# Splitting the state-space part of a fused layer into two column halves, and interleaving the phases of the halves

## The chip, the cores and the metric

One core of one Trainium2 chip. The metric is device microseconds of one execution. The kernel before takes 2095 to 2099 us (medians); executions of one kernel scatter by some 0.5%.

In the profile, PE is TensorE's matmuls, PEld its weight loads, DVE is VectorE, ACT is ScalarE, POOL is GpSimd and SP is SyncE, whose queue issues most transfers.

## The reference, cut to what matters

Forward and backward of a layer with two parallel branches on one normalised input, 2048 tokens wide 576 columns. All gradients are outputs.

```python
def _A_ref(u, ...):                       # state-space branch, N = 128, D = 576, L = 2048
    P = jnp.exp(logdA[:, :, None] * l[None, None, :])
    K = jnp.einsum("dn,dnl,dn->dl", Cc, P, dB).real
    ...                                   # y = irfft(rfft(u) * rfft(K)), plus u * Dskip
def _B_ref(x, W_gate, W_up, W_down):      # feed-forward branch, F = 4608
    gate = einsum(x, W_gate); up = einsum(x, W_up)
    return einsum(relu(gate) * up, W_down)
xn = _layernorm(x)
return x + _A_ref(xn, ...) + _B_ref(xn, ...)
# reference() returns the output and its vjp for all inputs
```

The state-space branch ("S4" below) treats every one of the 576 columns by itself. That is why it can be cut into two halves of 288 columns. The feed-forward branch ("FFN") is nearly all matmuls.

## The kernel before: the parts that the change and the argument touch

The FFN is a Python generator that yields an estimate of its own time after each piece. S4 is a second generator. The driver pulls S4 along so that its yields stay at `PACE` times those of the FFN. What is emitted earlier has priority; the compiler's scheduler then fixes each engine's order.

```python
PACE = 0.95
for us in ffn.gen(ln, final):
    ...
    ft += us
    while s4_open and stt < PACE * (ft - start):
        r = next(sgen, None)
        ...
        stt += r

def gen(self):                            # S4
    yield from self.phase1()              # transforms of signal and gradient -> dk
    yield from self.phase2()              # kernel K and its gradient sums: exp, sin, small matmuls
    yield from self.phase3()              # parameter gradients, transforms of K, products, transforms back
```

Phase 2 works on 144 groups of four columns; one group:

```python
v.tensor_tensor(E[:], ..., op=ALU.mult)
v.tensor_tensor(ya[:], ..., op=ALU.mult)
v.tensor_scalar(yr[:], ya[:], MAGIC, None, op0=ALU.add)
v.scalar_tensor_tensor(yr[:], yr[:], MAGIC, ya[:], op0=ALU.subtract, op1=ALU.subtract)
nc.scalar.activation(sn[:], yr[:], ACT.Sin, scale=-TWO_PI)
nc.scalar.activation(ya[:], yr[:], ACT.Abs)
nc.scalar.activation(cs[:], ya[:], ACT.Sin, scale=-TWO_PI, bias=g.hpcol[:])
v.tensor_tensor(Y[:, 0], Ef, cs[:], op=ALU.mult)
v.tensor_tensor(Y[:, 1], Ef, sn[:], op=ALU.mult)
...   # then 8 small matmuls, 8 transposes, 8 small matmuls, evictions, sums
```

The FFN's weight gradients read rows of the gradient (`gq`) and of the input (`xs`), in two buffers each:

```python
self.dp = pool("ffn_d", 2)
gq = self.dp.tile([P, ST, 144], BF16, name="gq")       # in dw_down, four per chunk
xs = self.dp.tile([P, ST, P], BF16, name="xs")         # in dw_gu and dw_left, five per chunk
```

## Time and profile before

| | before |
|---|---|
| time, median of 5 | 2095.1 us (2093.5 to 2102.7) |
| PE busy | 1870 us, 89% of the span |
| DVE, ACT busy | 1468 and 1465 us, 70% each |
| clock granted to PE | 0.968 |
| DMA packets, HBM | 239 thousand, 174 GB/s |

How to read it: no engine is full over the whole span, but each is nearly full somewhere. The page's slices, the table of stretches, the matmuls' true pace and PE's waits are in the prediction, which shows them line by line and works out that 1715 us of TensorE work are needed and some 378 us are lost.

### The profile page before, as it was taken

Reading aid. Unit: us, or ns where it says so; the run is one execution under the profiler, and the core shown is the slowest. Engines: PE = TensorE matmul, PEld = TensorE weight load, DVE = VectorE, ACT = ScalarE, POOL = GpSimd, SP = SyncE. Lnnn points to the kernel's source line nnn. Section 1 sums busy time; section 2 is a strip of 40 time slices with the busy share of each in tenths; the row PEclk is TensorE's granted clock in tenths of the full one; section 3 lists DMA queues with packets and bytes.
Section 4 is the critical chain, followed back from the end, with each engine's and each line's share of the span. In section 5 each row is a group of like instructions: output and inputs, shape, how many; then the busy total and the mean of one; then the engine's idle time right before and its main releaser. Section 6 shows DMA issues by size and latency. Waiting matters only on the chain.

```text
span 2092.8 us, 45262 instructions
## 1 busy us (share of the span) xinstructions
PE 1870.3 (89%) x17723; PEld 1279.1 (61%) x17723; DVE 1468.5 (70%) x3424; ACT 1465.3 (70%) x3187; POOL 263.3 (13%) x321
## 2 busy tenths in 40 slices
PE   6989999876899999989999999999898998899786
PEld 3655567544566666766666666666665674566455
DVE  6454555279999888898989878897356765741563
ACT  3665665468989988988979979888646762452562
POOL 4210100021111201201201101201101000010110
PEclk8999999987999999999999999999999998999988
DMA  9648789742555644645744735645857896995686
GB/s 306 223 155 297 219 249 290 221 113 53 113 126 119 130 114 108 134 117 109 141 119 108 159 94 109 138 128 99 246 156 228 243 284 240 306 268 149 173 238 185
DMA packets 239472, 366.60 MB, mean 175 GB/s; under 512 B 91866, under 2 KB 156506, under 8 KB 238490
## 3 DMA queue, kind: packets, MB, share of 16 engines
q1 hardware_dynamic: 207898, 297.64, 44.6%
q0 software_dynamic: 29248, 63.72, 19.3%
q8 instruction: 138, 2.26, 0.5%
q10 hardware_dynamic: 2112, 2.36, 0.3%
q14 instruction: 76, 0.62, 0.1%
HBM read 214.45 MB, written 149.20 MB: 174 GB/s over the span
## 4 chain that ended last, share of the span: by engine, by line
PE 37%; ACT 25%; DVE 17%; DMA 14%; issue 6%; SPq 1%; POOL 0%; ACTq 0%; DVEq 0%; POOLq 0%
PE ps_mm L246 8%; PE ps_mm L288 7%; PE ps_mm L322 6%; ACT osx L65 4%; ACT YT L65 3%; PE ps_s L603 3%; PE ps_mm L308 3%; DMA gq<-gq_dram 3%; PE ps_s L604 2%; ACT ysn L767 2%; ACT ycs L769 2%; ACT ya L768 2%; PE pt L270 2%; ACT hN L65 2%; DMA bC<-C_dk 1%
## 5 line engine op out<-in xcount | busy, mean ns | idle before, releaser
L65 ACT CAST osx<-ps_mm 128x288 bf16<-128x288 f32 x721 | 276.2, 438 | 61.8 <-PE ps_mm L288 59.4
L293 POOL DMA_DIRECT2D acc_dram<-osx x176 | 152.8, 871 | 1194.3 <-ACT osx L65 925.4
L288 PE MATMUL ps_mm<-wgT,dgT 128*128 128x288 bf16 x1152 | 218.2, 291 | 13.9 <-DVE upm L253 8.4
L288 PE MATMUL ps_mm<-wuT,duT 128*128 128x288 bf16 x1152 | 216.1, 290 | 0.0
L322 PEld LDWEIGHTS <-xs 128*128 128x128 bf16 x1536 | 147.9, 98 | 99.5 <-DMA xs<-xs_dram 5.4
L246 PE MATMUL ps_mm<-gT,wdT 128*128 128x512 bf16 x720 | 192.8, 386 | 10.0 <-DVE upm L253 10.0
L246 PE MATMUL ps_mm<-xT,wg 128*128 128x512 bf16 x720 | 199.8, 384 | 1.1 <-ACT osx L65 0.7
L308 PE MATMUL ps_mm<-gq,hN 128*128 128x144 bf16 x2304 | 172.6, 231 | 28.7 <-DMA gq<-gq_dram 28.7
L288 PE MATMUL ps_mm<-wd,hT 128*128 128x288 bf16 x1152 | 189.6, 289 | 8.3 <-ACT osx L65 2.6
L246 PE MATMUL ps_mm<-xT,wu 128*128 128x512 bf16 x720 | 193.1, 382 | 1.6 <-DVE upm L253 1.6
L308 PEld LDWEIGHTS <-hN 128*128 128x128 bf16 x2304 | 157.3, 100 | 37.5 <-DMA gq<-gq_dram 19.8
L253 DVE SCALAR_TENSOR_TENSOR upm<-rg,ps_mm 128x512 bf16<-128x512 bf16 x144 | 98.6, 685 | 112.6 <-PE ps_mm L246 89.1
L65 ACT COPY YT<-ps_s 128x1024 bf16<-128x1024 bf16 x143 | 148.6, 1039 | 17.3 <-PE ps_s L824 16.5
L322 PE MATMUL ps_mm<-dgN,xs 128*128 128x384 bf16 x768 | 144.8, 328 | 4.1 <-DMA xs<-xs_dram 4.1
L65 ACT CAST dhb<-ps_mm 128x512 bf16<-128x512 f32 x144 | 85.8, 596 | 82.4 <-PE ps_mm L246 82.0
L288 PEld LDWEIGHTS <-dgT 128*128 128x128 bf16 x1152 | 112.4, 99 | 46.0 <-issue 18.2
L322 PE MATMUL ps_mm<-duN,xs 128*128 128x384 bf16 x768 | 138.6, 326 | 0.0
L840 DVE TENSOR_TENSOR pr<-X,ps_s 128x256 f32<-128x256 f32 x288 | 110.5, 417 | 33.7 <-PE ps_s L836 33.2
L288 PEld LDWEIGHTS <-duT 128*128 128x128 bf16 x1152 | 113.6, 99 | 32.8 <-issue 2.3
L288 PEld LDWEIGHTS <-hT 128*128 128x128 bf16 x1152 | 108.3, 99 | 41.4 <-issue 8.1
L246 PEld LDWEIGHTS <-wdT 128*128 128x128 bf16 x720 | 70.2, 99 | 83.7 <-issue 14.8
L65 ACT CAST obw<-ps_mm 128x384 bf16<-128x384 f32 x103 | 48.9, 475 | 99.9 <-PE ps_mm L322 82.6
(247 smaller groups left out, 4141.6 us busy)
## 6 DMA issues: line engine op xcount, KB each, us to landing
acc_dram<-osx POOLq DMA_DIRECT2D x192, 288.0 KB, 4.8
gT<-gT_dram SPq DMA_DIRECT2D x44, 640.0 KB, 5.9
xT<-xT_dram SPq DMA_DIRECT2D x44, 640.0 KB, 5.6
gq<-gq_dram SPq DMA_DIRECT2D x48, 576.0 KB, 4.8
xs<-xs_dram SPq DMA_DIRECT2D x48, 512.0 KB, 3.9
A_ug<-fA SPq DMA_DIRECT2D x16, 576.0 KB, 4.1
out_dram<-obw SPq DMA_DIRECT2D x96, 96.0 KB, 2.7
b_ug<-A_ug SPq DMA_DIRECT2D x16, 576.0 KB, 5.6
```

Source lines behind the costliest of these rows:

```text
L65: self.nc.scalar.copy(out, in_)
L246: nc.tensor.matmul(ps[:], lhsT=w[:, k, fs], rhs=rhs[:, k, :], start=(k == 0), stop=(k == NK - 1))
L253: nc.vector.scalar_tensor_tensor(upm[:], rg[:], 0.0, ps_u[:], op0=ALU.is_gt, op1=ALU.mult)
L270: nc.tensor.transpose(out=pt[:, j, :], in_=src[:, j * P:(j + 1) * P], identity=g.ident_bf[:])
L288: nc.tensor.matmul(ps[:, :DH], lhsT=lt[:, js], rhs=rh, start=(i == 0), stop=(i == len(mms) - 1))
L293: nc.gpsimd.dma_start(g.acc_dram[:, t, :, :], o[:], accum_op=ALU.add)
L308: nc.tensor.matmul(ps[:, (ft - f) * 144:(ft - f + 1) * 144], lhsT=self.hN[:, st, ft * P:(ft + 1) * P], rhs=gq[:, st, :], start=(st == 0), ...
L322: nc.tensor.matmul(ps[:, :Fc], lhsT=xs[:, st, :], rhs=src[:, st, :], start=(st == 0), stop=(st == ST - 1))
L603: nc.tensor.matmul(ps[:, :DH], lhsT=CC[:], rhs=src[:, o, hs], start=True, stop=False)
L604: nc.tensor.matmul(ps[:, :DH], lhsT=sm[:], rhs=src[:, other, hs], start=False, stop=True)
L767: nc.scalar.activation(sn[:], yr[:], ACT.Sin, scale=-TWO_PI)
L840: nc.vector.tensor_tensor(pr[:], X[:, dx:dx + DG, r0:r0 + 2].rearrange("p d r a -> p d (r a)").unsqueeze(2).to_broadcast(sh), psg[:, 0:DG ...
```

## The change

Its intent is to spread S4's three phases, which load different engines, more evenly over the FFN. It does five things: (1) cut S4's arrays into halves; (2) mix phase 2 of one half with transforms of the other, and stretch the two pieces that have no partner; (3) write the transform matrices to DRAM and load slices of them; (4) let the row loads share three buffers; (5) shrink other pools to make room. The letters (a) to (e) of the prediction stand for other steps, and it leaves (3) out. The diff, cut to its core:

```diff
-PACE = 0.95
+PACE = 1.1
+W1, W2, W3 = 56.0, 400.0, 91.0
...
-        self.tp = pool("ffn_t", 2 * FTC)
+        self.tp = pool("ffn_t", 2 * FTC - 1)
-        self.dp = pool("ffn_d", 2)
+        self.dp = pool("ffn_d", 3)
...
-        gq = self.dp.tile([P, ST, 144], BF16, name="gq")
+        gq = self.dp.tile([P, ST, 144], BF16, name="rows")
...
-        xs = self.dp.tile([P, ST, P], BF16, name="xs")
-        nc.sync.dma_start(xs[:], g.xs_dram[k][:])
+        xs = self.dp.tile([P, ST, 144], BF16, name="rows")
+        nc.sync.dma_start(xs[:, :, 0:P], g.xs_dram[k][:])
...
-                per = (len(todo) + FTC - 1) // FTC
+                per = (len(todo) + FTC - 2) // (FTC - 1)
...
-        self.A = {1: d("A_k", [P, ST, 1, 2, D]), 2: d("A_ug", [P, ST, 2, 2, D])}
+        two = lambda name, shape: [d(f"{name}{hf}", shape) for hf in range(2)]
+        self.A = {1: two("A_k", [P, ST, 1, 2, DH]), 2: two("A_ug", [P, ST, 2, 2, DH])}
...   # phase1, phase2, phase3 become p1(hf), p2(hf, pools), p3(hf) on DH = 288 columns;
...   # dkc and yr get one buffer, YT two; the products of two spectra work in place
+    def both(self, a, wa, b, wb):
+        ta = tb = 0.0
+        for us in a:
+            ta += us
+            yield us
+            while b is not None and tb * wa < ta * wb:
+                r = next(b, None)
+                ...
+                    tb += r
+                    yield r
...
     def gen(self):
-        yield from self.phase1()
-        yield from self.phase2()
-        yield from self.phase3()
+        self.make_dft16()
+        yield 1.0
+        yield from self.make_dft128()
+        yield from self.params()
+        with ExitStack() as c:
+            pools = self.p2_pools(c)
+            for us in self.p1(0):
+                yield 2.5 * us
+            yield from self.both(self.p2(0, pools), 0.8 * W2, self.p1(1), W1)
+            yield from self.both(self.p2(1, pools), 0.8 * W2, self.p3(0), W3)
+        for us in self.p3(1):
+            yield 2.5 * us
+        yield from self.grads()
```

## The prediction

> **What bounds the kernel now.** Two programs share one core: a feed-forward part (FFN, twelve chunks of 384 columns) that lives on TensorE, and a state-space part (S4) in three phases: phase 1 (transforms of signal and gradient), phase 2 (the generated kernel, exponentials and sines), phase 3 (transforms back, parameter gradients). S4 is woven into the FFN by adding up estimated microseconds ("yields"). I began with the page's busy slices:
>
> ```profile
> PE   6989999876899999989999999999898998899786
> ...
> DVE  6454555279999888898989878897356765741563
> ACT  3665665468989988988979979888646762452562
> ```
>
> The reader should see three regimes, at 52 us a slice. In slices 9 to 28 VectorE and ScalarE are both nearly full: phase 2. Before and after (phases 1 and 3) they are half idle. TensorE is high everywhere but in slice 8, at the two ends and a little in the thirties. The busy times by stretch (us; then PE, PE weight loads, DVE, ACT, POOL busy; granted clock, DMA share, GB/s) make it exact:
>
> ```profile
> 150.00:450.00 300.00, 273.21 (x2212) 178.98 (x2210) 151.00 (x333) 172.99 (x418) 26.63 (x35) 0.98 0.80 246
> 450.00:500.00 50.00, 29.02 (x334) 21.09 (x335) 49.49 (x110) 41.56 (x81) 9.28 (x7) 0.70 0.28 53
> 500.00:1450.00 950.00, 890.02 (x9668) 627.61 (x9666) 841.13 (x1896) 844.11 (x1744) 125.08 (x128) 0.99 0.52 118
> 1450.00:1850.00 400.00, 358.47 (x2917) 236.34 (x2915) 239.21 (x590) 218.16 (x547) 30.42 (x36) 0.98 0.82 244
> 1850.00:1950.00 100.00, 97.40 (x898) 67.70 (x896) 28.06 (x61) 38.18 (x82) 9.97 (x12) 1.00 0.63 159
> 1950.00:2093.00 143.00, 105.14 (x856) 71.50 (x852) 73.75 (x160) 67.50 (x150) 11.62 (x14) 0.89 0.77 214
> ```
>
> Busy PE overstates, since matmuls overlap. So next I took the true pace of each kind of matmul from runs in the chain of waits (start, length, what, count) and from the PE timeline:
>
> ```profile
> 1867.00 2.81 PE ps_mm L246 x13
> 1869.80 2.21 PE ps_mm L288 x18
> ...
> 1882.41 6.01 PE ps_mm L308 x96
> ...
> 1902.99 10.40 PE ps_mm L322 x64
> ```
>
> ```profile
> 1012.77 0.35 PE L836 MATMUL ps_s<-dkc,YT 128*128 128x32 bf16 x8
> 1012.98 0.35 PE L815 MATMUL ps_s<-XC,Y 128*128 128x16 bf16 x8
> 1013.18 0.90 PE L288 MATMUL ps_mm<-wd,hT 128*128 128x288 bf16 x6
> 1014.24 0.61 PE L824 MATMUL ps_s<-ident_bf,Y 128*128 128x128 bf16 x8 [0.17 <-ACT Kst L65]
> 1014.68 0.53 PE L288 MATMUL ps_mm<-wgT,dgT 128*128 128x288 bf16 x3
> ```
>
> That is 0.216 us for 512 columns, 0.123 for 288, 0.0626 for 144, 0.1625 for 384, 0.055 for a 128-wide transpose (0.44 us for eight, start to start), 0.0255 for the tiny ones. Times the counts of the views by line: 2160 x 0.216 = 467; 4608 of 288 columns = 566 (3456 of the FFN, 1152 of S4); 2304 x 0.0626 = 144; 1536 x 0.1625 = 250; 3580 transposes = 197; 2304 tiny = 59; 1152 of 64 columns near 34. Together **about 1715 us of necessary TensorE time in 2093**. So 378 us are lost: waits, plus matmuls at half clock. The same count per stretch: 96 of the first 150 us; 245 of 300 (82%); 19 of 50 (39%); 842 of 950 (89%); 324 of 400 (81%); 95 of 100 in the FFN alone; 92 of the last 143. Phase 2 proper is the efficient regime, with three engines near 89% together; phases 1 and 3 and the seam at 400 to 500 us are the poor ones. PE's longest waits in total (us, times, longest):
>
> ```profile
> PE ps_mm L308 <- DMA gq<-gq_dram: 28.7, 12, 11.6
> PE pt L270 <- ACT hN L65: 20.4, 35, 6.6
> PE ps_s L636 <- DVE base L950: 16.1, 9, 4.0
> ```
>
> **What the Trainium skill says.** "Perfetto Trace Analysis", Identifying Performance Opportunities: where the most-contended engine changes over time, interleaving the regimes may help. That is this change's idea; the slices above show such regimes. The same section says matmul busy time is no measure of distance from the roofline; this trace agrees (1870 us busy, 1715 needed). "TensorE: Matmul & The Clock Gate", The HAM clock gate: an idle PE falls to half clock and must be busy again to regain it. It agrees: 0.70 granted in the stretch with most waiting, 0.98 to 1.00 in full ones. So a removed wait returns somewhat more than itself. "DMA: Bandwidth & Descriptors", Why small descriptors are slow: a fixed overhead per packet. Packets here took 59 ns at 1152 B and 30 ns at 576 B, so halving rows to 576 B is free; 256 B packets took 18 ns, so 4096 B as sixteen packets costs 288 instead of 211.
>
> **The change, part by part.**
> (a) S4 is split into two column halves of 288. Phase 1 of half 0 goes first, its pace stretched by 2.5; then phase 2 of half 0 mixed with phase 1 of half 1; then phase 2 of half 1 mixed with phase 3 of half 0; then phase 3 of half 1, stretched; then parameter gradients. The matmuls and PSUM evictions keep their number and their 288 columns. VectorE gains instructions: 48 products of 5 operations become 96 at half width, and the base additions also split; a product over 1152 elements took 0.754 us and one over 576 took 0.453, so an instruction costs 0.15 us before its elements; some 270 more make 41 us, spread over the run and half of it inside the mixed part. PE gains nothing.
> (b) Adding the yields: FFN 120.6 a chunk, so 69 after chunk 0, and 1396 before the last section. Phase 2 was 788, and at pace 0.95 it spread over 827 FFN units. Now both mixed parts are 452 + 487 = 939, at pace 1.1: 854 units. Phase 1 alone took 121 units; half of it now gets 127. Phase 3 was 221 units; its second half with the gradients gets 240. S4's emission ends at unit 1299 instead of 1243; the last section starts near 1340, so no flush.
> (c) The mixed part is denser. Phase 2's own work sums in the trace to 911 us of DVE and 626 of ACT. The half phases add about 92 us of products and base additions and 336 evictions of some 0.42 us. With overlap, the two engines' 1841 busy us of the present phase 2 (0.885 x 1040 x 2) become near 2050, and PE's need over those units 1.10 times. The ratio DVE/ACT to PE stays nearly one, so I expect the same 88 to 89% and no new single bound.
> (d) gq and xs buffers, two each, become three shared ones. Today the third gq load of a chunk waits for the first one's matmuls, then takes 4.8 us while 3 us of matmuls remain. With three, the next loads are ahead by two. I count 25 of the 28.7 us as removed.
> (e) Smaller pools for yr, dkc, YT, hT: dkc alone can bite (POOL copies of 1.1 + 1.5 us in the view of that tile, once per 32 columns, 18 times, within a group period near 5.8 us): 0 to 15 us lost.
>
> The sum, keeping 1715: first 150 us unchanged; mixed stage about 1010 us of need / 0.885 = 1141; remaining 421 us of need / 0.87 = 484 (before 82%; relieved of the seam, of the base additions' 16 us and of the C loads' 10, both at half rate or mixed); tail 243 - 11 for the gq wait in it = 232. Total 2007. I add 15 for dkc, the doubled number of phase seams, and the first groups of phase 2, which will again make PE wait: **2022 us**, 0.965 of before.
>
> **Rivals.** (1) Phase 2 is really bound by DVE plus ACT, and mixing more into it lengthens it by the full 1.11 (2050/1841): 1040 becomes 1155; if phases 1 and 3 then stay at 82%, 421 / 0.82 = 513, total 150 + 1155 + 513 + 243 = 2061. For it: both engines at 89%. Against: phase 3's PE waits on DVE vanish when spread. (2) The two PSUM banks of S4 become the limit: phase 2's groups and the transforms' evictions now alternate in them, and an in-order PE behind a taken bank stops the FFN too. The trace already has 13.6 us of PE waiting for the Kst eviction. If such waits triple, +30 to 50 us: 2050 to 2070. (3) The SP queue, which waits in order, gets some 300 more issues at 0.32 us, and loads come late: +20. (4) The mixing is better than I think, 91% throughout from 150 to 1850: (1715 - 96 - 187) / 0.91 = 1574, total 1957.
>
> **Range and chances.** 2007 to 2022 is my centre; rivals 1 and 2 reach 2061 to 2070, rival 4 1957. Range 1970 to 2075. 2% is 2053: faster by over 2% 0.72, within 2% 0.24, slower 0.04.
>
> **What would show it.** Right: no slice of PE near 6 or 7 between the ends, but for the start of phase 2; DVE and ACT slices at 8 to 9 over some 22 slices, with lower ones before and after; waits on gq (now "rows") under 8 us; S4's mixed stage from about 340 to 1480 us; the wait on base gone. Wrong: PE waits on ACT's Kst or YT, or on DVE's pr, growing past 60 us together (rival 2); DVE over 93% in the mixed stage with PE below 86% (rival 1); DMA waits on S4's half loads among the top five (rival 3); a flush of S4 at the end, which would leave the tail longer than 243 us.

## The result, and the profile after

| | before | after |
|---|---|---|
| time, median | 2096.7 us (16 runs) | 2023.4 us (9 runs, 2014.9 to 2027.2) |
| ratio to before | | 0.9639, 95% interval 0.9615 to 0.9662 |
| PE busy | 1870 us | 1848 us |
| PE idle (span less busy) | 223 us | 174 us |
| clock granted to PE | 0.968 | 0.978 |
| DMA packets | 239 thousand | 390 thousand |

A ratio here and below is the mean time of one kernel's runs over that of the kernel before's runs of the same rounds, so it is not quite the ratio of the medians.

It is 3.6% faster. First the busy slices of the changed kernel, 51 us each:

```profile
PE   6989897999999999999999999999999999988786
...
DVE  7454593498989888897988988989883654545662
ACT  3664673698889889989989988887985653554562
```

In the kernel before PE's slices 8 to 11 (counted from 1; the prediction counts from 0), around the start of phase 2, read 8, 7, 6, 8, and 8s followed at the 18th, 29th, 31st, 34th and 35th; here everything from the 8th slice to the 34th is a 9. The lowest slice between the two ends is now the seventh (303 to 354 us), a 7. DVE and ACT are nearly all at 8 to 9 from the 9th slice to the 30th, where before it was the 10th to about the 28th: the dense stage became longer, since it took in more work. The stretches of the changed kernel (length; PE, PEld, DVE, ACT, POOL busy with counts; granted clock, DMA share, GB/s):

```profile
150.00:300.00 150.00, 137.77 (x1023) 86.46 (x1021) 99.08 (x275) 91.91 (x219) 10.27 (x16) 0.98 0.77 209
300.00:350.00 50.00, 40.51 (x391) 31.33 (x389) 19.38 (x55) 20.05 (x49) 4.26 (x5) 0.93 0.87 229
350.00:1500.00 1150.00, 1087.02 (x11418) 761.90 (x11417) 993.96 (x2355) 1003.39 (x2179) 144.79 (x148) 0.99 0.67 162
1500.00:1850.00 350.00, 326.70 (x2782) 222.72 (x2780) 174.28 (x527) 185.90 (x439) 27.67 (x32) 0.98 0.78 202
1850.00:1950.00 100.00, 83.70 (x634) 51.55 (x633) 60.18 (x141) 55.87 (x125) 11.45 (x14) 0.92 0.86 239
1950.00:2022.00 72.00, 51.29 (x517) 38.37 (x515) 25.87 (x54) 24.05 (x54) 3.45 (x4) 0.90 0.68 192
```

I counted the needed TensorE time again, with the prediction's durations and the instructions that start in each stretch: 1714 us over all, so the work is the same. (The traces have 3654 matmuls of 128 columns where the prediction counted 3580; with these the sum is 1721 us in both kernels.) The need is 103 us in the first 150, then 123, 35, 1024, 307, 76 and 46 us in the rows above. The long mixed stage reaches 1024 / 1150 = 89.0%. The 50 us at which phase 2 began before, with 19 us needed and DVE 99% busy, have no counterpart now.

PE's longest waits in the changed kernel (us in total, times, longest; hN holds the FFN's activations after their transposes, fA the result of the first step of a transform, C the data before the last step of a transform back, base the sum that phase 3 stores, Kst the kernel K, upm a product in the FFN):

```profile
PE pt L271 <- ACT hN L66: 17.2, 23, 7.1
PE ps_mm L309 <- DMA rows<-gq_dram: 11.0, 3, 7.7
PE ps_s L640 <- DMA bC<-C_dk: 10.5, 6, 5.8
PE ps_s L599 <- ACT fA L66: 10.4, 18, 1.8
```

Against the list of before: the wait for gq rows fell from 28.7 to 11.0 us (that for xs rows rose from 4.1 to 6.1), the wait of the transforms back for base from 16.1 to 0.3. What is left is spread: 10.6 of the 17.2 us for hN and 13.8 us for rows lie after 1850 us, 8.0 of the 10.5 us for the C loads and 6.4 of the 10.4 us for fA in the unmixed piece before 350 us.

### The profile page after: what moved, and what is told of

Same layout as the page of the kernel before. It is cut to its first block, busy times and chain, and to the rows that moved or that the text cites.

```text
span 2021.7 us, 46212 instructions
## 1 busy us (share of the span) xinstructions
PE 1847.8 (91%) x17723; PEld 1273.5 (63%) x17723; DVE 1456.8 (72%) x3647; ACT 1467.3 (73%) x3242; POOL 256.5 (13%) x321
## 5 line engine op out<-in xcount | busy, mean ns | idle before, releaser
L323 PEld LDWEIGHTS <-rows 128*128 128x128 bf16 x1536 | 148.2, 98 | 101.6 <-DMA rows<-xs_dram 6.3
L247 PE MATMUL ps_mm<-xT,wg 128*128 128x512 bf16 x720 | 204.4, 387 | 3.1 <-ACT osx L66 2.6
L247 PE MATMUL ps_mm<-gT,wdT 128*128 128x512 bf16 x720 | 188.4, 385 | 6.8 <-DVE upm L254 5.9
L309 PE MATMUL ps_mm<-rows,hN 128*128 128x144 bf16 x2304 | 161.3, 230 | 11.0 <-DMA rows<-gq_dram 11.0
L309 PEld LDWEIGHTS <-hN 128*128 128x128 bf16 x2304 | 152.5, 100 | 14.4 <-DMA rows<-gq_dram 10.7
L323 PE MATMUL ps_mm<-dgN,rows 128*128 128x384 bf16 x768 | 143.7, 328 | 6.1 <-DMA rows<-xs_dram 6.1
L323 PE MATMUL ps_mm<-duN,rows 128*128 128x384 bf16 x768 | 140.1, 326 | 0.0
L810 ACT ACTIVATE ysn<-yr 128x512 bf16<-128x512 f32 x144 | 95.5, 663 | 29.4 <-DVE yr L807 27.0
```

The source lines that it names most:

```text
L247: nc.tensor.matmul(ps[:], lhsT=w[:, k, fs], rhs=rhs[:, k, :], start=(k == 0), stop=(k == NK - 1))
L309: nc.tensor.matmul(ps[:, (ft - f) * 144:(ft - f + 1) * 144], lhsT=self.hN[:, st, ft * P:(ft + 1) * P], rhs=gq[:, st, :], start=(st == 0), ...
L323: nc.tensor.matmul(ps[:, :Fc], lhsT=xs[:, st, 0:P], rhs=src[:, st, :], start=(st == 0), stop=(st == ST - 1))
```

## The experiments

The theory: TensorE's need sets the time, and the gain comes from mixing phases that load different engines, which removes stretches where TensorE starves. The rivals: the gain is the row buffers; it is only the longer spread of S4; it is the smaller pieces; VectorE and ScalarE are the real bound of the dense stage. Every kernel below gave correct results, and each "median" stands beside the kernel before's of the same session (2096 to 2099 us). The traces of experiments 1 to 8 lack 138 to 152 matmul records each, all of 512 columns and spread over the span, so busy PE is a little too low there.

**1. The row buffers alone.** The kernel before, with

```diff
-        self.dp = pool("ffn_d", 2)
+        self.dp = pool("ffn_d", 3)
-        gq = self.dp.tile([P, ST, 144], BF16, name="gq")
+        gq = self.dp.tile([P, ST, 144], BF16, name="rows")
-        xs = self.dp.tile([P, ST, P], BF16, name="xs")
+        xs = self.dp.tile([P, ST, 144], BF16, name="rows")
```

> The kernel before with the three shared row buffers alone. My step (d) counts 25 us for them: 2070 us, ratio 0.988. But the trace after has lost 15 us of gq waits between 150 and 1950 us and kept 14 us of row waits in the tail, so that reading says 2081, ratio 0.993. Rival, that the buffers are most of the gain: under 2050, ratio under 0.978. PE's wait for the gq rows should fall from 28.7 us to under 15.

Measured: 2093.3 us, ratio 0.9983 (0.9967 to 1.0000). A miss: nearly nothing. PE's waits of this kernel, from the top of the list:

```profile
PE pt L270 <- ACT hN L65: 26.6, 46, 6.4
PE ps_s L824 <- ACT Kst L65: 17.3, 37, 1.7
PE ps_s L636 <- DVE base L950: 16.1, 11, 3.4
PE ps_mm L288 <- DVE upm L253: 14.5, 4, 8.4
```

The 28.7 us for gq, first in the list before, have become 5.5 us. But the wait for hN rose from 20.4 to 26.6 us, that for Kst from 13.6 to 17.3, that of the output matmuls for upm from 8.4 to 14.5, and that for xs rows from 4.1 to 9.2. The buffers did what they should, and the time did not follow: other waits grew by at least as much (all of PE's waits in the list sum to 215 us, after 208). A part is the edit's own: the xs rows now land in pieces of 256 B, and their loads took 4.5 us instead of 3.9, so this run is not the third buffer alone.

**2. The smaller pools alone.** The kernel before, with

```diff
-        self.tp = pool("ffn_t", 2 * FTC)
+        self.tp = pool("ffn_t", 2 * FTC - 1)
-                per = (len(todo) + FTC - 1) // FTC
+                per = (len(todo) + FTC - 2) // (FTC - 1)
-            ytp = self.pool(c, "k_yt", 3)
+            ytp = self.pool(c, "k_yt", 2)
+            yp1 = self.pool(c, "k_y1", 1)      # for yr
-                    dkc = xop.tile(...)
+                    dkc = parp.tile(...)       # one buffer instead of two
```

> The kernel before with the smaller pools alone (five tiles instead of six for the transposed activations with their fewer slots, one dkc, one yr, two YT). My step (e): 0 to 15 us lost, 2096 to 2111 us, ratio 1.000 to 1.007. If the smaller pools are costly (over 20 us, ratio over 1.010), the mixing has to gain more than I said.

Measured: 2092.1 us, ratio 0.9977 (0.9965 to 0.9990). They cost nothing; the change could afford to give them up.

**3. Halves, but one phase after the other.** The changed kernel, with

```diff
-PACE = 1.1
+PACE = 0.923
-            for us in self.p1(0):
-                yield 2.5 * us
-            yield from self.both(self.p2(0, pools), 0.8 * W2, self.p1(1), W1)
-            yield from self.both(self.p2(1, pools), 0.8 * W2, self.p3(0), W3)
-        for us in self.p3(1):
-            yield 2.5 * us
+            yield from self.p1(0)
+            yield from self.p1(1)
+            yield from self.p2(0, pools)
+            yield from self.p2(1, pools)
+            yield from self.p3(0)
+        yield from self.p3(1)
```

> The changed kernel with the halves one after another in the old order of phases (phase 1 of both, phase 2 of both, phase 3 of both, nothing stretched), the pace set so that the state-space part still ends at the same unit (0.923). If the mixing of regimes is the cause, most of the gain goes: 2065 to 2095 us, ratio 0.985 to 1.000. Rival, that half-width pieces, smaller transfers and shared row buffers are the cause: 2020 to 2040, ratio 0.965 to 0.973.

Measured: 2124.8 us, ratio 1.0133 (1.0093 to 1.0173), outside both expected ranges. The whole gain is gone, and 28 us more. Its PE and DVE slices (53 us each):

```profile
PE   6898998998958899999999999999989779878876
...
DVE  7444782344999989888898889899347536645663
```

The low slice is back where phase 2 starts, at 583 us, with DVE full beside it. The stretch around it:

```profile
580.00:660.00 80.00, 47.79 (x556) 33.47 (x557) 76.56 (x171) 59.69 (x111) 7.47 (x5) 0.72 0.18 52
```

For 80 us VectorE is 96% busy, PE 60%, and the clock granted to PE is 0.72. PE's waits of this kernel:

```profile
PE ps_s L640 <- DVE base L728: 23.1, 15, 3.4
...
PE ps_s L640 <- DMA bC<-C_dk: 15.0, 10, 2.9
...
PE ps_s L640 <- DMA bC<-C_ydu: 12.4, 6, 3.2
PE ps_s L599 <- ACT fA L66: 12.2, 15, 1.7
```

These four sum to 63 us. In experiment 4 (whole width, same end of S4) the same four sum to 27 us:

```profile
PE ps_s L636 <- DVE base L950: 12.7, 10, 3.9
...
PE ps_s L636 <- DMA bC<-C_dk: 7.7, 13, 1.3
...
PE ps_s L636 <- DMA bC<-C_ydu: 3.9, 2, 2.1
...
PE ps_s L590 <- ACT fA L65: 2.3, 5, 1.1
```

Unmixed, the changed kernel is therefore 43 us slower than the whole-width one. Twice as many small steps that each wait for a load or an eviction would explain it, but this is not shown to be the cause: the run also loads the transform matrices in slices, for which weight loads waited 15.2 us here and never in experiment 4, and has other pools and another pace.

**4. The kernel before at a slower pace.** `PACE = 0.907` instead of 0.95, nothing else.

> The kernel before at pace 0.907, so that its state-space part ends at unit 1299 as in the changed one. Mixing theory: the later end alone gives little, 2080 to 2100 us, ratio 0.992 to 1.002. Rival, that the gain is only the longer spread of the state-space part: under 2050, ratio under 0.978.

Measured: 2082.1 us, ratio 0.9922 (0.9899 to 0.9945). So at this setting a slower pace, with S4 ending later, gained 15 us without any mixing. It is one setting; experiment 12 shows how much one can mislead.

**5. Mixing without stretching.** The changed kernel, with `yield from self.p1(0)` and `yield from self.p3(1)` in place of the two loops with 2.5, and pace 0.924 so that S4 ends at the same unit.

> The changed kernel with both mixed parts kept, but the first and the last piece no longer stretched by 2.5; pace 0.924, so that the state-space part ends at the same unit (the mixed parts then take 1017 units instead of 854). If mixing phase 2 with the transforms is the cause, it stays within 15 us of the changed kernel: 2010 to 2040 us, ratio to before 0.959 to 0.973. If the stretching of the two unmixed pieces carries the gain, 2050 or more, ratio over 0.978.

Measured: 2054.7 us, ratio 0.9804 (0.9772 to 0.9836). It is outside what I expected of mixing alone, and in the range of the other case, that the stretching carries a part. The difference to the change is 31 us (2054.7 less 2023.4). The table of lost time below places it: 15 us more are lost in the first part of the run and 18 in the third, where the two pieces without a partner lie, and 4 in the tail, against 8 won in the middle. The named waits do not show it: those for fA and the C loads sum to 23 us here and to 27 in the changed kernel. The run changes two things, since the slower pace also spreads the mixed parts over 1017 units instead of 854; that the stretching alone is worth 31 us is not shown.

**6. More VectorE work.** The changed kernel, in each phase-2 group

```diff
                         v.tensor_tensor(Y[:, 0], Ef, cs[:], op=ALU.mult)
+                        v.tensor_tensor(Y[:, 0], Ef, cs[:], op=ALU.mult)
```

> The changed kernel with one VectorE product of each phase-2 group done twice: 144 x 0.43 = 62 us more VectorE work, same result. If the mixed stage is bound by the engines together (my 89% everywhere), a third to two thirds of it shows: 2043 to 2065 us. If VectorE is the single bound (rival 1): 2075 or more. If VectorE has slack: under 2035.

Measured: 2027.8 us, ratio 0.9679 (0.9652 to 0.9706). Its busy times:

```profile
PE 1832.3 (90%) x17578; PEld 1267.7 (63%) x17723; DVE 1498.8 (74%) x3791; ACT 1467.2 (72%) x3242; POOL 255.9 (13%) x321
```

VectorE's busy time rose by 42 us (from 1456.8; neighbouring instructions overlap, so the 62 us shrink to 42), and the time by 4 us by the medians or 8 by the ratios. VectorE, 86% busy in the mixed stage, does not bind it. My expectation of a joint bound missed.

**7. More TensorE work.** The changed kernel, with each of the eight transposes of a group done twice:

```diff
                 nc.tensor.transpose(out=tb[:, i * P:(i + 1) * P], in_=Y[:, ri, dl, :], identity=g.ident_bf[:])
+                nc.tensor.transpose(out=tb[:, i * P:(i + 1) * P], in_=Y[:, ri, dl, :], identity=g.ident_bf[:])
```

> The changed kernel with the eight transposes of each phase-2 group done twice: 144 x 8 x 0.055 = 63 us more TensorE work, same result. My count takes TensorE's need as what sets the time: at least 80% of it shows, 2073 to 2095 us. If DVE and ACT set the time in the mixed stage and TensorE only fills: under 2055.

Measured: 2082.7 us, ratio 0.9926 (0.9904 to 0.9948). Of the 63 us added, 59 show. The matmul count is 18,725 in a trace that again lacks some. With experiment 6 this shows which engine sets the time where phase 2 runs: TensorE far more than VectorE.

**8. The tail's row loads on another queue.** In the changed kernel's tail PE waits twice for rows (start, length, what, count, and the idle time before with its cause):

```profile
1963.16 9.16 PE L309 MATMUL ps_mm<-rows,hN 128*128 128x144 bf16 x144
1979.99 5.18 PE L309 MATMUL ps_mm<-rows,hN 128*128 128x144 bf16 x48 [7.67 <-DMA rows<-gq_dram]
1991.28 3.99 PE L323 MATMUL ps_mm<-dgN,rows 128*128 128x384 bf16 x14 [6.12 <-DMA rows<-xs_dram]
```

and the SP queue shows the fourth gq load issued late, behind the loads and stores of the final tiles:

```profile
1968.88 0.38 SPq L985 DMA_DIRECT2D f_acc<-acc_dram  x1
...
1973.68 0.34 SPq L991 DMA_DIRECT2D out_dram<-f_o  x1
1974.11 0.46 SPq L300 DMA_DIRECT2D rows<-gq_dram  x1
```

Its buffer was the first of the three, free once the first 48 of the 144 matmuls that began at 1963 were done. The edit, in the three row loads, with `self.last` set for the last section:

```diff
-        nc.sync.dma_start(gq[:], g.gq_dram[q][:])
+        (nc.gpsimd if self.last else nc.sync).dma_start(gq[:], g.gq_dram[q][:])
```

> The changed kernel with the row loads of the last section issued from the GpSimd queue instead of the SP queue, where they stand behind the final tiles' loads and stores. The tail has 14 us of TensorE waits for rows; if the queue is the cause, 8 to 14 us go: 2009 to 2016 us, ratio to before 0.958 to 0.961. If the loads are late for their buffers or for the DMA engines, no change: 2019 to 2027.

Measured: 2013.5 us (2011.4 to 2014.5), ratio 0.9609 (0.9582 to 0.9635). The same place after the edit:

```profile
1962.92 9.16 PE L310 MATMUL ps_mm<-rows,hN 128*128 128x144 bf16 x144
1978.57 4.82 PE L310 MATMUL ps_mm<-rows,hN 128*128 128x144 bf16 x48 [6.49 <-DMA rows<-gq_dram]
1983.23 1.95 PE L324 MATMUL ps_mm<-dgN,rows 128*128 128x384 bf16 x11
```

The wait for xs is gone; that for the fourth gq load shrank by only 1 us. GpSimd issued it at 1970.0, after an accumulating store and 4 us earlier than SP had, but the matmuls that need it began only 1.4 us earlier: in this run the gq loads of GpSimd's queue took 6.9 us to land, those of SP's 5.0 (medians). From the 144 matmuls at 1963 to the end it is 49.2 us, after 58.5. The version beats both kernels by the medians (10 us; 6 by the ratios); its interval and the changed kernel's overlap, so about 0.3% is likely, not certain.

**9. More VectorE work in the kernel before.** The edit of experiment 6 in the kernel before.

> The kernel before with the same VectorE product done twice, 144 x 0.43 = 62 us, all of it now in the unmixed phase 2 where VectorE is 89% busy. The changed kernel hid 54 of these 62 us. If VectorE bound phase 2 before and the mixing relieved it, 35 to 62 us show: 2130 to 2160. If it had slack there too, so that the mixing gained elsewhere: under 2112, ratio under 1.007.

Measured: 2107.4 us, ratio 1.0056 (1.0023 to 1.0089). Busy VectorE rose by 47 us, the time by 9 to 12. VectorE had slack in the unmixed phase 2 as well, although it was 89% busy there. The gain of the change is therefore not the relief of an overfull VectorE along phase 2. It may matter at the seam, where it is 96 to 99% busy; no run tests it there alone. From 450 to 500 us of the kernel before, the chain of work that ended last runs through ScalarE for 53% and through VectorE for 31%; from 580 to 660 us of experiment 3 it is 26% and 54%.

**10. More ScalarE work.** The changed kernel, with `nc.scalar.activation(sn[:], yr[:], ACT.Sin, scale=-TWO_PI)` done twice in each group.

> The changed kernel with one ScalarE sine of each phase-2 group done twice: 144 x 0.63 = 91 us more ScalarE work, same result. If ScalarE is hidden behind TensorE as VectorE was: under 2040. If ScalarE, which carries most evictions that TensorE waits for, is a second bound: 2060 to 2110.

Measured: 2044.2 us, ratio 0.9737 (0.9720 to 0.9754), between the two expectations. Busy ScalarE rose by 64 us (1467.3 to 1530.8), the time by 21: a third. ScalarE does most of the evictions that PE waits for, which fits that more of its added work shows than of VectorE's.

**11. More buffers in the last loop of phase 1.** Experiment 8 with `f"p1_c{hf}", 5` instead of 3.

> The tail version (2013.5 us) with five instead of three buffers in the last loop of phase 1. That loop's C loads made TensorE wait 10.5 us, nearly all in the unmixed half. If the number of loads in flight is the cause, 5 to 10 us go: 2004 to 2009, ratio 0.956 to 0.959. If the loads wait for the stores of the loop before, no change: 2011 to 2016.

Measured: 2014.9 us, ratio 0.9595 (0.9573 to 0.9616). No change against experiment 8 beyond the scatter, and the wait for the C loads stayed: 9.7 us after 10.2. The number of buffers is not its cause; that the loads wait for the stores of the loop before fits, but was not tested.

**12. The same at pace 1.07.**

> The same at pace 1.07 instead of 1.1, so that the state-space part ends at unit 1332, just before the last section at 1340. The kernel before gained 15 us from ending 56 units later. If the changed one still has room, 5 to 10 us less than the run without: about 2000. If its S4 work now runs into the final tiles, 5 to 20 us more.

Measured: 2058.3 us, ratio 0.9816 (0.9787 to 0.9846). It is 43 us worse than at 1.1, against both expectations. The waits are spread over many stages, none of them large; the passage from the first mixed part to the second near 800 to 1000 us lost 9 us more than in experiment 11, the end from 1800 us some more. I have no single cause, and this stays open. It warns that single settings of the pace, 15 us better in one kernel and 43 worse in another, may partly be luck. Experiments 3, 4 and 5 have one setting each, and no run varies the pace around them.

Put in a row (each step is one path through the edits; the buffers of 1 and 2 and the loaded matrices come in between the second and third, and the pace changes at the first four steps):

| kernel | median us | step |
|---|---|---|
| before | 2097.4 | |
| before, pace 0.907 (4) | 2082.1 | -15 |
| halves, unmixed (3) | 2124.8 | +43 |
| halves, mixed, not stretched (5) | 2054.7 | -70 |
| mixed and stretched: the change | 2023.4 | -31 |
| tail's rows on another queue (8) | 2013.5 | -10 |

The size of each step is uncertain, since one change of pace moved a time by 43 us; the gain of mixing and stretching together, 101 us, is well above that. The kept traces say where. Cut at the start of the 144-column matmuls of the 4th, 9th and 12th chunk of the FFN, and with the need of the prediction's durations subtracted (missing records counted in), they give this estimate of lost TensorE time:

| lost us, by part of the run | first: to chunk 4 | middle: 4 to 9 | third: 9 to 12 | tail | all |
|---|---|---|---|---|---|
| before | 169 | 80 | 104 | 15 | 368 |
| before, pace 0.907 (4) | 155 | 67 | 120 | 14 | 356 |
| halves, unmixed (3) | 184 | 63 | 130 | 20 | 396 |
| mixed, not stretched (5) | 141 | 75 | 87 | 23 | 326 |
| the change | 126 | 83 | 69 | 19 | 297 |

The middle, where phase 2 runs in all of them, is not better in the change. The gain lies in the first part, which has phase 1 and the seam, and in the third, which has phase 3. Experiment 12 against 11 loses 11, 16, 33 and 3 us more in the four parts.

## Why the prediction was right, point by point

The time was right to 2 us (2022 predicted, 2023.4 measured). That it was so close is luck: the terms are off by up to 22 us, and their errors cancel. Lost time is the length of a stage less TensorE's need in it:

| lost TensorE time, us | predicted | after |
|---|---|---|
| first 150 us | 54 | 47 |
| mixed stage | 131 (1141 - 1010) | 126 (1150 - 1024) |
| the stages beside it | 63 (484 - 421) | 85 (550 - 465) |
| allowance for dkc, seams, first groups | 15 | 0 |
| tail | 46 (232 - 186) | 50 (172 - 122) |
| sum | 309 | 308 |

- **1715 us of need set the time.** Right. The recount gives 1714, and added TensorE work came through at 94% (experiment 7).
- **(a) Halving keeps the PE work and costs little.** Half right. The work stayed. But the step only counted VectorE's instructions, and their 41 us did not show: VectorE's busy time fell by 12 us (1468.5 to 1456.8). Unmixed, the changed kernel was 43 us slower than the whole-width one (experiment 3 against 4), with longer waits for loads and evictions; how much of this is the halves is open. With the mixing it did not show in the sum.
- **(b) The units and the order.** Right: the last phase-2 sums end at 1517 us (I had said about 1480), the transforms back at 1778 and the parameter gradients at 1851, before the final tiles start at 1882.
- **(c) The mixed stage at 88 to 89%.** Right in size, 89.0%, wrong in the reason. I took three engines near 89% for a joint bound. Experiments 6, 9 and 10 show that VectorE has slack there (42 us of busy time cost 4 to 8) and ScalarE some (64 cost 21). What remains is TensorE with many short waits.
- **(d) 25 us for the three row buffers.** Wrong as a gain. Alone they gave 0.2%. Of the 28.7 us, 17.7 went away in the changed kernel (the 11.0 left are more than the 8 named as a sign of being right), but in experiment 1 such a gain was taken up by other waits. The 11 us of it that I put into the tail failed for another reason: there the loads were late in the SP queue, not for want of a buffer (experiment 8).
- **(e) 0 to 15 us for the smaller pools.** It was none, or a slight gain (experiment 2).
- **The first groups of phase 2 would again make PE wait.** Wrong: in the change this seam is gone. Unmixed it is back. This is the term that paid for the 22 us too few in the unmixed stages.
- **The stages beside it at 87%.** Too high: 84.5%. At 200 to 250 us and 300 to 350 us TensorE needs only 35 of 50 us, waiting for evictions of fA and for the C loads.
- **Rivals.** Rival 1 (VectorE and ScalarE bind) fell with experiments 6 and 9. Rival 2 (two PSUM banks): the wait for Kst halved, 13.6 to 6.9 us, instead of tripling. Rival 3 (SP queue): its sign came, the loads of S4's halves are among the five longest waits (C loads, 10.5 us); but before they had cost 10.0, and late issues are shown in the tail alone. Rival 4 (91% throughout) did not come.

## What to carry to other kernels

Count the pipelined engine's need from start-to-start distances and compare it stage by stage with the clock; then mix the poor stages with the rich ones, and stretch what has no partner. An engine that is 86 to 89% busy in a stage need not bind it: double one of its instructions and see how much comes through. Removing the longest wait of a list may return nothing, because the next waits grow, so test such a step alone before adding its microseconds to a sum. And take more than one setting of a pace before you trust the size of a step.

## What the Trainium skill lacked or had wrong

- "Perfetto Trace Analysis", Identifying the Most-Contended Engine, takes occupancy of VectorE and ScalarE as a fair measure of how near they are to their roofline, judges TensorE by LDWEIGHTS busy and the share of its peak, and names the engine of highest occupancy as the most contended. It has no test of whether that engine binds. In the mixed stage VectorE (994 of 1150 us) and ScalarE (1003) were busy 86 and 87%, TensorE's weight loads 66% (762), yet 42 us more VectorE work cost 4 to 8 us and 64 us more ScalarE work 21, while 63 us more TensorE work cost 59. A doubled instruction told what occupancy did not.
- The same page, Optimization Strategy, on interleaving regimes: borne out (70 us between experiments 3 and 5, with a single pace each), but the section does not say that what makes the interleaving possible can cost something first: 43 us between experiments 4 and 3.
- "DMA: Bandwidth & Descriptors", Issuing engines are not separate DMA queues, says that issuing from several engines only saves the sequencer's issue time. Here it also let a load pass others that stood ahead of it in one queue: with the last section's row loads on GpSimd's queue a wait of 6.1 us vanished, and the median fell by 10 us (6 by the ratios).
- The same page, Why small descriptors are slow: the overhead is seen in the loads (the row loads in pieces of 256 B landed in 4.5 us where they had taken 3.9), but the page does not say when it costs a kernel anything. In experiment 1, 92 thousand more packets (239 to 332) went with an unchanged time (ratio 0.9983).
- No page has it: a change of 3% in the emission pace moved the time by 43 us (experiment 12), without one wait that explains it.
